# Weight conversion in a fused RWKV-7 and feed-forward kernel: two pieces land in another buffer, six conversion steps stand earlier, nine exponents are made by ScalarE

## The chip, the cores and the metric

The kernel runs on one core of a Trainium2 chip. The metric is the device time of one execution in microseconds (us), the median of the runs shown. The core has five instruction queues that matter here: TensorE (PE, matrix products), VectorE (DVE), ScalarE (ACT), GpSimd (POOL), and SyncE (SP), which issues nearly all DMAs. Each queue works through its instructions in the order written.

## The reference

An RWKV-7 recurrence (4 batches, 8 heads, 768 steps, head size 40) feeds a feed-forward block with a hard-swish (3072 tokens, width 320, hidden 2048):

```
for t in range(S):
    kt, vt, rt = (k[:, :, t], v[:, :, t], r[:, :, t])
    wt, at, bt = (w[:, :, t], a[:, :, t], b[:, :, t])
    y[:, :, t] = np.einsum('bhd,bhde->bhe', rt, state)
    Sa = np.einsum('bhde,bhe->bhd', state, at)
    state_decay = state * wt[:, :, None, :] - np.einsum('bhd,bhe->bhde', Sa, bt)
    state = state_decay + np.einsum('bhd,bhe->bhde', vt, kt)
...
x = np.ascontiguousarray(attn_out.transpose(0, 2, 1, 3)).reshape(B * S, H * D)
h = x @ w_in
relu6 = np.clip(h + 3.0, 0.0, 6.0)
g = h * relu6 / 6.0
return (g @ w_out).astype(np.float32)
```

The six inputs of the recurrence are float32. The two weights `w_in` (320 x 2048) and `w_out` (2048 x 320) arrive as float64, so the kernel has to turn 1.3 million doubles into floats before it can use them.

## The kernel before

**The work.** The sequence is cut into blocks of 64 steps. A *unit* is one block of two batches; there are 24 units (`NK`), handled in groups of four (`NU`). For each unit, preparatory stages (`W`, `gam`, `A`, `B`, `F`, `K`, `factor`, `E`, `EV`) make decay products and score matrices; one inversion per group (`invert`) makes the inverses of many small triangular matrices on VectorE (`prod`, `x`, then the transposes `tb`, `tt`), completed by `third_block` on TensorE (through `zs`) into the tile `tinv`; then the unit's steps (`RT`, `VT`, `C`, `R`, `S`, `U`, `UT`, `rS`, `sn`, `H`, `y`) run the recurrence over the block, and `move`/`move2` carry the result `yg` by DMA into the tile `xt`. The feed-forward reads `xt`: `expand` (L1051, weight `win` and `win2`, products in `h`) and, behind the activation `gt` (ScalarE L1066, VectorE L1067), `contract` (L1092, weight `wout`).

**The conversion.** The weights come in 20 pieces of 128 x 512 doubles, numbered from 0 here; each is 512 KB and is loaded raw as pairs of 32-bit words. `load_weights` is a generator. For piece n it issues, as four steps: (1) the exponent: VectorE keeps the top 12 bits of the high word in the tile `parts` (L349), and two ScalarE instructions make a power of two of them (L350, L352); (2) the product of the piece before, n-1, into its place in `win`, `win2` or `wout` (L360); (3) the mantissa bits of the high word, in place (L369); (4) the low word added (L373). `parts` has two buffers, used in turn. Pieces 0 to 9 are one half of the hidden columns, 10 to 19 the other. The raw words need a home of 1024 words a partition: `raw_homes` lists one for each piece, and for some the number of an earlier piece that must be done before the home is free (`free`). The DMAs of a piece (L327) are issued by SP as soon as its home is free in that sense.

**What sets the order.** The order on every queue is written out by hand. For the first inversion, conversion steps are dealt at fixed steps of the inversion (`STEPS`). The four units of the first group then follow the table `PLAN`: an entry such as `3UT:10` runs stage `UT` of unit 3 and deals ten conversion steps after its matrix products are issued and before its evacuation is; `X` and `Y` are the two halves of the third blocks. What the plan does not deal is dealt in later entries, so the sequence of steps is fixed and the plan only sets what stands between them. The second group's preparation (`by_twos`) begins with the plan's eleventh line.

The lines that matter, as the profile numbers them: L327 raw loads; L349, L350, L352, L360, L369, L373 conversion; L517 masked scores; L541 and L552 scans of the decay; L534 and L538 copies that feed the scans; L954 state update; L980 `ys`; L917 evacuation of `UT`; L880 evacuation of `S`; L995 and L1000 the moves into `xt`; L806 the copies into `tinv`.

Of the kernel before, what the change touches and what calls it, by code (L numbers as in the profile page):

```python
# [7 lines left out]

F32 = mybir.dt.float32
I32 = mybir.dt.int32  # L10
U32 = mybir.dt.uint32
ALU = mybir.AluOpType
AF = mybir.ActivationFunctionType
# [3 lines left out]
P = 128  # L17
BL = 64
# [3 lines left out]
EXP = 916  # L22
# [8 lines left out]
def kernel(  # L31
# [42 lines left out]
    nc = tc.nc  # L74
# [7 lines left out]
    NH = NU * H  # L82
# [4 lines left out]
    const = ctx.enter_context(tc.tile_pool(name="const", bufs=1))  # L87
# [3 lines left out]
    inv = ctx.enter_context(tc.tile_pool(name="inv", bufs=1))  # L91
# [48 lines left out]
    def ps_pair(*dims):  # L140
# [21 lines left out]
        out=ident[:], in_=ones, pattern=[[1, P]],  # L162
# [4 lines left out]
        out=ones[:, 0:BL], in_=ones[:, 0:BL], pattern=[[1, BL]],  # L167
# [3 lines left out]
        out=ones[BL:P, 0:BL], in_=ones[BL:P, BL:P], pattern=[[1, BL]],  # L171
# [6 lines left out]
    nc.vector.memset(three[:], 3.0)  # L178
    warm = const.tile([P, 1], F32, name="warm")
    nc.scalar.activation(out=warm[:], in_=three[:], func=AF.Relu)  # L180
    low = const.tile([P, 2], F32, name="low")
    for i, x in enumerate((EXP - 1792.0, -1792.0 * 2 ** 23)):
        nc.vector.memset(low[:, i:i + 1], x)


# [35 lines left out]
    for i in range(3):  # L221
        t = const.tile([P, H, BL], F32, name=f"score{i}")
# [14 lines left out]
    for p in range(NP):  # L237
        t = const.tile([P, 2, NPR, SLOT], F32, name=f"state{p}")
        nc.vector.memset(t[:], 0.0)
        state.append(t)  # L240
        t = const.tile([P, 2, NPR], F32, name=f"last{p}")
# [16 lines left out]
    for i, (x, y) in enumerate([(0, DFF // 2), (0, NJ // 2)]):  # L258
        for n, z in enumerate((x, y)):
            t = win[:, :, z:z + H * SLOT] if i == 0 else \  # L260
                wout[:, z:z + 4, :].rearrange("p j m -> p (j m)")[:, 0:2 * H * SLOT].rearrange(
                    "p (n x) -> p n x", n=2)
            t = t.rearrange("p n (h e) -> p n h e", e=SLOT)
            name = ("WA", "BK")[i][n]
# [3 lines left out]
    for u in range(2):  # L268
        t = win2[:, u * NPR * P:(u + 1) * NPR * P]
        placed["rgam", 2 + u] = t.rearrange("p (r t) -> p r t", t=P)  # L270
    WC = 256
    PIECES = 20
# [4 lines left out]
    def raw_homes():  # L277


        raws = inv.tile([P, NH, BL], F32, name="raw", tag="F", bufs=2)  # L280
        raws = raws[:].rearrange("p h t -> p (h t)").bitcast(U32)
        places = [raws[:, n * 4 * WC:(n + 1) * 4 * WC] for n in range(2)]
        for j in (NJ // 4, 3 * NJ // 4):
            places.append(wout[:, j:j + NJ // 4, :].rearrange("p j m -> p (j m)")[:, 0:4 * WC].bitcast(U32))
        places = [x.rearrange("p (n c t) -> p n c t", n=2, t=2) for x in places]
        for c in (DFF // 4, 3 * DFF // 4):
            x = win[:, :, c:c + 2 * WC].bitcast(U32)
            places.append(x.rearrange("p n (c t) -> p n c t", t=2))
        x = tinv[:].rearrange("p h t -> p (h t)").bitcast(U32)
        for n in range(2):  # L290
            y = x[:, n * 4 * WC:(n + 1) * 4 * WC]
            places.append(y.rearrange("p (n c t) -> p n c t", n=2, t=2))
        a, b, c, d, e, f, g, h = places
        order = [g, h, a, b, c, d, e, f, a, b, c, d, "x", "fb", "tt", a, b, "fb", "tt", a]
        free = [None] * 8 + [2, 3, 4, 5, None, None, None, 8, 9, 13, 14, 15]
        left = {}
        for n, (x, before) in enumerate(zip(order, free)):
            if isinstance(x, str):
                if x not in left:
                    left[x] = inv.tile([P, L, L], F32, name=f"raw_{x}", tag=x)  # L300
                x = left[x][:].rearrange("p t s -> p (t s)").bitcast(U32)
                x = x.rearrange("p (n c t) -> p n c t", n=2, t=2)
            yield x, before

    def load_weights():

        todo, homes = weight_pieces(), raw_homes()
        loaded, done, issued = deque(), [], [0]
        upcoming = []

        def load():
            if issued[0] == min(PIECES, limit[0]):
                return False
            if not upcoming:
                upcoming.append(next(homes))
            raw, before = upcoming[0]  # L320
            if before is not None and before not in done:
                return False
            upcoming.clear()
            issued[0] += 1
            out, loads = next(todo)
            for to, src in loads(raw):
                nc.sync.dma_start(out=to, in_=src)  # L327
            loaded.append((out, raw))
            return True

        while load():
            pass
        refill.append(load)
        phase[0] = 0
        yield
        before = None
        parts = [grp.tile([P, HD + WPAD], F32, name=f"parts{n}", tag="KBt", bufs=NU + 2)
                 for n in range(2)]
        parts = [t[:, 0:2 * WC].bitcast(U32).rearrange("p (n c) -> p n c", n=2) for t in parts]
        for n in range(PIECES + 1):  # L340
            now = None
            if n < PIECES:
                while load():
                    pass
                out, raw = loaded.popleft()
                hi = raw[:, :, :, 1]
                x = parts[n % 2]
                now = out, raw, x
                nc.vector.tensor_scalar(x, hi, 0xFFF00000, None, ALU.bitwise_and)  # L349
                nc.scalar.activation(out=x.bitcast(F32), in_=x.bitcast(I32), func=AF.Prelu, bias=low[:, 0:1],  # L350
                                     scale=-2.0 ** -20, alpha=2.0 ** -40)
                nc.scalar.activation(out=x.bitcast(I32), in_=x.bitcast(F32), func=AF.Prelu, bias=low[:, 1:2],  # L352
                                     scale=-2.0 ** 63, alpha=2.0 ** -40)
                phase[0] = 1
                yield
            if before:
                to, m, yf = before
                if len(to.shape) == 4:
                    m, yf = (z.rearrange("p n (j c) -> p n j c", c=to.shape[3]) for z in (m, yf))
                nc.vector.tensor_tensor(out=to, in0=m, in1=yf, op=ALU.mult)  # L360
                converted[0] += 1
                done.append(n - 1)
                while load():
                    pass
                phase[0] = 2
                yield
            before = None
            if now:
                nc.vector.tensor_scalar(hi, hi, 0xFFFFF, 0x100000, ALU.bitwise_and, ALU.bitwise_or)  # L369
                phase[0] = 3  # L370
                yield
                m = hi.bitcast(F32)
                nc.vector.scalar_tensor_tensor(m, raw[:, :, :, 0], 2.0 ** -32, hi, ALU.mult, ALU.add)  # L373
                before = out, m, x.bitcast(F32)
                phase[0] = 4
                yield
# [780 lines left out]
    third, F, group_F = [], None, []  # L1157
# [65 lines left out]
    n, cleared = 0, []  # L1223
# [19 lines left out]
    def block(i, j):  # L1243

        if i % NU < 2:
            if j == 0:
# [5 lines left out]

    PLAN = """X X:2 0U:4 0UT:2 1R
              0sn:2 0H:1 Y:2
              1U 1UT:2 0y
              2RT:1 Y:1
              1sn:1 1H:1 2VT:2 0move 0move2
              1y:2 2R
              2S:3 3RT:2
              1move 1move2 2U:3 2UT:1 2C:5  # L1260
# [193 lines left out]
```

## Time and profile before

| | us |
|---|---|
| median of 3 runs | 799.37 (797.80 to 799.43) |
| profiled execution | 800.17 |
| its span, first to last instruction | 798.4 |
| TensorE busy | 734.0 (92%) |
| VectorE busy | 500.5 (63%) |
| ScalarE busy | 307.1 (38%) |
| GpSimd busy | 177.1 (22%) |

The profiled execution is 0.80 us above the median, and 1.8 us of it lie outside its span. TensorE is busy nearly all the time from 140 us on; before that the shares change from stage to stage, so the stages have to be read one by one. A piece of conversion shows in the profile as one line of each of L349, L350, L352, L360, L369 and L373.

### The profile page before, as it was taken

What the parts mean: (1) busy time and instruction counts of PE and PEld (TensorE: products, weight loads), DVE (VectorE), ACT (ScalarE), POOL (GpSimd) and SP (SyncE); (2) the same over time, 40 slices, a digit from 0 to 9 for tenths busy, and PEclk for the clock granted to TensorE, in tenths of its full rate; (3) what the DMA queues carried; (4) which work ended last, traced back from release to release, by engine and by line L of the source; (5) the groups of instructions that cost most, each with busy time, mean ns of one, the idle gap of its engine ahead of it and who ended that gap; (6) DMA issues with size and microseconds to landing.
All of it is one profiled execution on the core that took longest, in us unless ns stands there. A gap on an engine that the chain in (4) does not pass through costs nothing.

```text
span 798.4 us, 35296 instructions
## 1 busy us (share of the span) xinstructions
PE 734.0 (92%) x15832; PEld 624.0 (78%) x15832; DVE 500.5 (63%) x986; ACT 307.1 (38%) x648; POOL 177.1 (22%) x318
## 2 busy tenths in 40 slices
PE   5726778999999989999999999999999999999998
PEld 4625667878778878788888888888888888888886
DVE  7898877689546699445798355888444983323210
ACT  2337653222553424452334454334444324412111
POOL 6403012421223313123214123304222202000000
PEclk9855798999999999999999999999999999999999
DMA  9693653420324322233212223213222101110000
GB/s 122 113 202 87 155 140 55 78 46 9 57 51 72 62 44 39 44 62 59 45 40 42 49 54 63 50 30 62 40 51 45 24 16 29 30 25 13 14 19 17
DMA packets 174214, 45.02 MB, mean 56 GB/s; under 512 B 157424, under 2 KB 172784, under 8 KB 174064
## 3 DMA queue, kind: packets, MB, share of 16 engines
q1 hardware_dynamic: 169760, 42.03, 27.8%
q8 instruction: 125, 2.05, 1.1%
q10 hardware_dynamic: 4304, 0.74, 0.7%
q14 instruction: 25, 0.20, 0.1%
HBM read 34.08 MB, written 3.93 MB: 48 GB/s over the span
## 4 chain that ended last, share of the span: by engine, by line
PE 77%; DVE 8%; issue 5%; SPq 5%; DMA 3%; ACT 1%; POOL 1%; POOLq 0%; DVEq 0%; ACTq 0%
PE h L1051 27%; PE o L1092 23%; PE pair L509 4%; PE pair L969 3%; SPq L455 3%; PE one L471 2%; PE pair L946 2%; PE pair L481 2%; PE pair L853 2%; PE pair L891 2%; PE pair L687 1%; PE pair L911 1%; PE pair L927 1%; PE one L875 1%; SPq L452 1%
## 5 line engine op out<-in xcount | busy, mean ns | idle before, releaser
L1051 PE MATMUL h<-xt,win 128*128 128x128 f32 (+1 forms) x2304 | 252.6, 284 | 3.2 <-DVE gt L1067 2.7
L1051 PEld LDWEIGHTS h<-xt,win 128*128 128x128 f32 (+1 forms) x2304 | 232.9, 193 | 20.6 <-issue 5.4
L1092 PE MATMUL o<-wout,gt 128*128 128x320 f32 x768 | 230.2, 443 | 0.0
L1092 PEld LDWEIGHTS o<-wout,gt 128*128 128x128 f32 x768 | 138.3, 190 | 50.2
L1067 DVE SCALAR_TENSOR_TENSOR gt<-gt,h 128x512 f32<-128x512 f32 x96 | 62.0, 682 | 71.2 <-ACT gt L1066 71.0
L1066 ACT ACTIVATE gt<-h,three 128x512 f32<-128x512 f32 x96 | 62.2, 686 | 101.6 <-PE h L1051 101.2
L981 POOL TENSOR_TENSOR yg<-ys,gam 128x512 f32<-128x512 f32 x22 | 39.7, 1803 | 162.6 <-DVE ys L980 71.8
L738 DVE TENSOR_TENSOR prod<-x 128x30 f32<-128x30 f32 (+9 forms) x180 | 67.2, 373 | 8.8 <-POOL x L723 3.3
L660 POOL TENSOR_TENSOR KBt<-K,rgt 128x320 f32<-128x320 f32 x22 | 19.1, 866 | 212.3 <-ACT rgt L649 207.4
L744 DVE TENSOR_TENSOR x<-x,prod 128x30 f32<-128x30 f32 (+9 forms) x180 | 62.3, 346 | 5.4
L954 DVE TENSOR_TENSOR state<-pair,state 40x320 f32<-40x320 f32 (+1 forms) x44 | 21.4, 487 | 65.5 <-PE pair L946 39.2
L517 DVE COPY_PREDICATED score<-mask,pair 128x512 f32<-128x512 int32 x71 | 50.0, 723 | 1.7 <-PE pair L509 1.2
L980 DVE TENSOR_TENSOR ys<-pair,ys 128x512 f32<-128x512 f32 x22 | 15.2, 690 | 40.9 <-PE pair L687 21.7
L552 DVE TENSOR_TENSOR_SCAN wm<-wm,start 128x528 f32<-128x528 f32 x24 | 37.6, 1566 | 0.8
L541 DVE TENSOR_TENSOR_SCAN prods<-wm,start 128x528 f32<-128x528 f32 x24 | 30.1, 1260 | 10.2 <-ACT wm L538 10.1
L831 ACT ACTIVATE RT<-pair 128x512 f32<-128x512 f32 x21 | 12.5, 597 | 52.8 <-PE pair L481 52.7
L692 ACT ACTIVATE EV<-pair 64x320 f32<-64x320 f32 x44 | 19.0, 432 | 33.7 <-PE pair L687 23.1
L806 ACT ACTIVATE tinv<-pair 32x256 f32<-32x256 f32 x48 | 18.0, 375 | 30.1 <-PE pair L796 29.4
L569 POOL COPY gam<-prods 128x256 f32<-128x256 f32 x24 | 22.5, 938 | 30.6 <-DVE prods L541 26.7
L1110 ACT ACTIVATE ob<-o 128x320 f32<-128x320 f32 x22 | 9.6, 435 | 49.4 <-PE o L1092 29.6
L969 PE MATMUL pair<-score,KBt 64*64 64x64 f32 x1472 | 27.4, 221 | 1.1 <-DVE state L954 0.9
L969 PEld LDWEIGHTS pair<-score,KBt 64*64 64x64 f32 x1472 | 24.0, 134 | 3.7 <-DVE state L954 1.4
(262 smaller groups left out, 1061.6 us busy)
## 6 DMA issues: line engine op xcount, KB each, us to landing
V<-in_v_dram SPq DMA_DIRECT2D x96, 40.0 KB
out_dram<-ob SPq DMA_DIRECT2D x47, 80.0 KB
R<-in_r_dram SPq DMA_DIRECT2D x92, 40.0 KB
B<-in_b_dram SPq DMA_DIRECT2D x42, 80.0 KB
K<-in_k_dram SPq DMA_DIRECT2D x42, 80.0 KB
W<-in_w_dram SPq DMA_DIRECT2D x37, 80.0 KB
A<-in_a_dram SPq DMA_DIRECT2D x37, 80.0 KB
xt<-yg SPq DMA_DIRECT2D x72, 40.0 KB
```

Source lines behind the costliest of these rows:

```text
L509: nc.tensor.matmul(out=o[i][half(q), n, :], lhsT=lhs[half(i, D), n ^ (2 * q * swap), half(q)], rhs=rhs[half(i, D), n, half(q)], start=True ...
L517: nc.vector.copy_predicated(out=x[:].rearrange("p (i h) t -> p i h t", i=2), mask=mask8, data=o[2])
L541: nc.vector.tensor_tensor_scan(out=prods[:].rearrange("p r m i -> p (r m i)"), data0=wm[:, 0:SCAN], data1=start[:], initial=0.0, op0=ALU.m ...
L552: nc.vector.tensor_tensor_scan(out=back, data0=back, data1=start[:], initial=0.0, op0=ALU.mult, op1=ALU.add)
L738: nc.vector.tensor_tensor(out=pv, in0=_ap(x[:], (i + 1) * L + i, [[L, n], [0, i]]), in1=_ap(x[:], i * L, [[0, n], [1, i]]), op=ALU.mult,)
L744: nc.vector.tensor_tensor(out=rest, in0=rest, in1=pv, op=ALU.add)
L969: nc.tensor.matmul(out=y[q][half(s), pr, :], lhsT=o[name][half(q), h * D:h * D + SLOT], rhs=m[name][half(q), 4 * rs + 2 * s + j, :], start ...
L981: nc.gpsimd.tensor_tensor(out=yg[:], in0=m["ys"][:].rearrange("p r q t -> p r (q t)"), in1=o["G"][:], op=ALU.mult)
L1051: nc.tensor.matmul(out=hp[c][:, i, :], lhsT=lhsT, rhs=rhs, start=(begun[c] == 0), stop=(begun[c] == 3 * NQ - 1))
L1066: nc.scalar.activation(out=gt[:], in_=hp[c][:], func=AF.Relu, bias=three[:], scale=1.0)
L1067: nc.vector.scalar_tensor_tensor(out=gt[:], in0=gt[:], scalar=6.0, in1=hp[c][:], op0=ALU.min, op1=ALU.mult)
L1092: nc.tensor.matmul(out=op[:], lhsT=gts[c][:, n, :], rhs=wout[:, c * HJ + r * NQ + n, :], start=((split or r == 0) and c == 0 and n == 0), ...
```

## The change

Three edits, all in the conversion.

1. Pieces 15 and 16 get homes in a new tile `more` that takes the place of the first group's `F`. Pieces 17 and 18 take the two homes in `raw` (free once pieces 8 and 9 are done), piece 19 the home in `fb` (free once piece 13 is done). Before, pieces 15, 16 and 19 were in `raw` (behind 8, 9 and 15), 17 in `fb` (behind 13) and 18 in `tt` (behind 14).
2. In the plan, three conversion steps are dealt behind the products of `y` of unit 0 (before: none), and four behind those of `sn` of unit 1 (before: one).
3. For pieces 0 to 3 and 15 to 19, ScalarE makes the exponent field itself: it reads the top 16 bits of each double as an integer, multiplies by 1/16 and subtracts 15/32, and writes the result as an integer into `parts`. The VectorE instruction L349 of these pieces goes.

```
-    low = const.tile([P, 2], F32, name="low")
-    for i, x in enumerate((EXP - 1792.0, -1792.0 * 2 ** 23)):
+    low = const.tile([P, 3], F32, name="low")
+    for i, x in enumerate((EXP - 1792.0, -1792.0 * 2 ** 23, -15.0 / 32.0)):
...
-        order = [g, h, a, b, c, d, e, f, a, b, c, d, "x", "fb", "tt", a, b, "fb", "tt", a]
-        free = [None] * 8 + [2, 3, 4, 5, None, None, None, 8, 9, 13, 14, 15]
+        order = [g, h, a, b, c, d, e, f, a, b, c, d, "x", "fb", "tt", 0, 1, a, b, "fb"]
+        free = [None] * 8 + [2, 3, 4, 5, None, None, None, None, None, 8, 9, 13]
...
+            if isinstance(x, int):
+                if x == 0:
+                    more = inv.tile([P, NH, BL], F32, name="more", tag="F", bufs=2)
+                    more = more[:].rearrange("p h t -> p (h t)").bitcast(U32)
+                x = more[:, x * 4 * WC:(x + 1) * 4 * WC].rearrange("p (n c t) -> p n c t", n=2, t=2)
...
-                nc.vector.tensor_scalar(x, hi, 0xFFF00000, None, ALU.bitwise_and)
+                fine = 2.0 ** -20
+                if n < 4 or n >= PIECES - 5:
+                    fine = 1.0
+                    top = raw.rearrange("p n c t -> p n (c t)").bitcast(I16)[:, :, 3::4]
+                    nc.scalar.activation(out=x.bitcast(I32), in_=top, func=AF.Identity, bias=low[:, 2:3],
+                                         scale=1.0 / 16.0)
+                else:
+                    nc.vector.tensor_scalar(x, hi, 0xFFF00000, None, ALU.bitwise_and)
                 nc.scalar.activation(out=x.bitcast(F32), in_=x.bitcast(I32), func=AF.Prelu, bias=low[:, 0:1],
-                                     scale=-2.0 ** -20, alpha=2.0 ** -40)
+                                     scale=-fine, alpha=2.0 ** -40)
...
-              1U 1UT:2 0y
+              1U 1UT:2 0y:3
...
-              1sn:1 1H:1 2VT:2 0move 0move2
+              1sn:4 1H:1 2VT:2 0move 0move2
```

The order of TensorE's and GpSimd's instructions is the same in both kernels. VectorE has nine conversion instructions fewer and one constant more, ScalarE nine activations more. SP issues the loads of pieces 15 to 17 ahead of unit 0's move, piece 18 behind it and piece 19 behind unit 1's, where before piece 15 followed unit 0's move, piece 16 unit 1's, and 17 to 19 came behind the first loads for the second group.

More of the change, by code (lines that the diff above doesn't have):

```diff
@@ L9 @@
 F32 = mybir.dt.float32
+I16 = mybir.dt.int16
 I32 = mybir.dt.int32
```

## The prediction

> **What bounds the kernel now.** I read the page's slices first, then TensorE's timeline from 60 to 135 us, then VectorE's and ScalarE's for what ends each gap, then the stretches of 1 us for the granted clock.
>
> ```profile
> PE   5726778999999989999999999999999999999998
> DVE  7898877689546699445798355888444983323210
> ACT  2337653222553424452334454334444324412111
> PEclk9855798999999999999999999999999999999999
> ```
>
> Each digit is 20 us. From the eighth slice on TensorE is full at full clock; nothing in the change touches that part, so time can only be won or lost before about 135 us and is then carried to the end. In slices three to seven VectorE is nearly full and TensorE's clock is low. TensorE's last waits in this stage (start, duration, then the wait and its releaser):
>
> ```profile
> 108.39 1.16 PE L1051 MATMUL h<-xt,win 128*128 128x128 f32 x8 [2.06 <-DVE gt L1067]
> 113.16 0.69 PE L911 MATMUL pair<-tinv,RR 64*64 64x64 f32 x32 [2.07 <-DVE ys L980]
> 121.93 1.08 PE L471 MATMUL pair<-ident,WA 128*128 128x128 f32 x4 [3.60 <-issue]
> 131.41 1.34 PE L969 MATMUL pair<-score,KBt 64*64 64x64 f32 x64 [0.87 <-DVE state L954]
> ```
>
> Three of the four are the conversion's doing. VectorE waits for a raw piece with `ys` behind it, and again for the next:
>
> ```profile
> 111.14 0.43 DVE L349 TENSOR_SCALAR parts<-raw 128x512 uint32<-128x512 uint32 x1 [2.21 <-DMA raw<-in_moe_w_out_dram]
> 112.41 0.69 DVE L980 TENSOR_TENSOR ys<-pair,ys 128x512 f32<-128x512 f32 x1
> 115.24 0.43 DVE L349 TENSOR_SCALAR parts<-raw_fb 128x512 uint32<-128x512 uint32 x1 [1.54 <-DMA raw_fb<-in_moe_w_out_dram]
> 122.83 2.39 DVE L541 TENSOR_TENSOR_SCAN prods<-wm,start 128x528 f32<-128x528 f32 x2
> ```
>
> And ScalarE reaches `UT` of unit 3, whose bank the product at 121.93 needs (that is the "issue" wait), only behind the last piece:
>
> ```profile
> 120.62 0.72 ACT L352 ACTIVATE parts<-parts,low 128x512 int32<-128x512 f32 x1
> 121.25 0.58 ACT L917 ACTIVATE UT<-pair 128x512 f32<-128x512 f32 x1
> ```
>
> From 122.83 VectorE then runs without a break to the score at 131.26: two scans, two more (L552), `gt`, `state`. It sets the product at 131.41. So the figure to forecast is when that scan chain starts.
>
> **Part by part.**
>
> *Pieces 0 to 3.* Each loses a L349 worth 0.33 us of VectorE's pitch (39.22 to 39.56) and adds 0.74 us on ScalarE (pitch of L350 to L352, 50.68 to 51.42). The new read is of 16-bit integers with a stride; no row has that. Bounds: the contiguous 32-bit row of the same 512 elements, 0.72 us, and twice that, 1.44 us, if the stride cost a second pass. I take 0.72, the nearest row. Two savings vanish: L369 of piece 1 now has to wait until ScalarE has read the high words (50.68 + 0.72 = 51.40, against L369 at 51.43 before), and the score at 52.13 already waited 0.28 us for products that hang on the load of `R`. So only piece 2's 0.33 us reaches the transposes at 62.18. Piece 3's new activation then stands on ScalarE ahead of the copies into `tinv` (L806, 69.13), which release the next products: 69.13 - 0.33 + 0.74 = 69.54. This edit makes TensorE 0.41 us later from 70.4 on.
>
> *The plan's six steps.* They fill VectorE's waits of 1.97 us (before 79.92) and 2.62 us (before 84.91). Ahead of the first come L369, L373 and L349, 1.3 us; ahead of the second, with what stood there, work that ends at 84.3 against products ready at 85.3. Both fit. On ScalarE piece 7's two activations pass ahead of `RT` of unit 2 and the second L806 (+1.2 us, not needed until 89.8). The rest of the conversion is 4.6 us of VectorE's idle time nearer its end. In my walk through the queues, ScalarE's `RT` of unit 2 (behind piece 11) makes the products at 93.55 start at 94.45, but `U` no longer waits, so the feed-forward starts at 97.5 for 97.17: +0.33.
>
> *The loads.* Pieces 15 to 17 (512 KB each) go ahead of unit 0's move on SP: three issues of some 0.5 us each, and SP starts 0.4 later, so the move ends its first four issues at 94.1 for 92.2. The transfers ahead hold 1.5 MB; at the 300 to 380 GB/s of the busiest stretches that is 4 to 5 us from 90, so `xt` lands near 96.5, 1 us before it is read. The waits of 2.21 and 1.54 us for raw pieces go. SP is later by 2 us for piece 19 (107.3); with the 5 us that raw pieces took (105.6 to 111.1) it lands at 113, needed at 113.9. The loads for unit 5 follow by 112.3, in place of 110.2, needed at 118.6.
>
> *Pieces 15 to 19 on ScalarE.* A piece is now 0.75 + 0.75 + 0.65 = 2.15 us there. Piece 15 starts at 101.6 (behind `VT`), then `ys` at 103.75, piece 16 to 106.4, piece 17 to 108.6, `S`, and only then `gt` at 109.1, which started at 106.93 before. Queued behind the pieces: `gt` on VectorE and the products at 108.39, now 110.35. This is the price, 2.0 us, and TensorE is idle from 106.7: 3.7 us.
>
> Then it pays. VectorE is through piece 16 by 107.3 and stands free: `ys` follows its products at once. TensorE at half clock from 110.4: 4.0 us for `h` and `score`, `ys` done at 114.95, `UT`'s products at 115.0 (113.16 before, all still late by 1.85). But ScalarE does piece 18 from 110.3, `U`, piece 19 from 113.9, and `UT` at 116.1 in place of 121.25. TensorE goes through to 118.65 without a gap and takes the product of 121.93 there, at full clock: done at 119.25. The copy for the second scan (L538) follows at 119.95, the second scan starts at 120.0 for 124.03 and the chain behind it is 4.05 us earlier: `state` at 126.8, the product of 131.41 at 127.35.
>
> *The clock.* The rows that decide it:
>
> ```profile
> 111.00:112.00 1.00, 0.08 (x8) 0.00 (x0) 0.86 (x2) 0.40 (x1) 0.00 (x0) 1.00 0.94 124
> 112.00:113.00 1.00, 0.00 (x0) 0.00 (x0) 1.00 (x3) 0.97 (x3) 0.00 (x0) 1.00 0.66 163
> 114.00:115.00 1.00, 1.00 (x26) 0.88 (x17) 0.00 (x0) 0.00 (x0) 0.83 (x1) 0.50 1.08 383
> 121.00:122.00 1.00, 0.07 (x1) 0.10 (x2) 0.90 (x2) 1.00 (x4) 0.00 (x0) 0.50 0.00 0
> ```
>
> The second and third numbers are TensorE's busy time and its weight loads'; the last three are granted clock, DMA share, GB/s. The clock changes at 93.4, 100.2, 113.9, 117.2, 120.8 and 127.4, all near multiples of 3.4 us apart, and falls after a stretch of that length with 1.0 to 1.4 us of work; with 2.0 us it held once (107 to 110.4) and fell once (at 172). After the change TensorE, fast, has done its work by 124.5 and waits 2.85 us for `state`; the stretch 124.1 to 127.5 holds 0.5 us of work, so I expect half clock to 130.9: 1.7 us lost.
>
> Sum: -4.05 + 1.7 = -2.35 us. The profiled execution would be 797.8; taken from the median, 799.37 - 2.35 = 797.0.
>
> The Trainium skill (TensorE: Matmul & The Clock Gate, section "HAM oscillation") gives the rule that no idle gap should exceed about 3.4 us. By it the 2.85 us gap would cost nothing and the time would be 795.3; but the trace lost the clock at 113.9 after gaps no longer than 2.07 us, and the row decides.
>
> **The rivals.**
>
> *The clock holds* at 127.5: -4.05, 795.3. For it: 1.5 us more of work in that stretch may be enough (2.0 us held it once). Against: the gap is long.
>
> *The clock eats it*: a stretch with 2.3 us of work (93.4 to 96.8) did not bring the clock back, so half clock may last two stretches, 3.4 us: -0.65, 798.7. The change also would come to this if `more` held up `xt`.
>
> *Slower: ScalarE's queue.* If the strided 16-bit activation takes 1.44 us, piece 3 delays `tinv` by another 0.72, and pieces 15 to 17 delay `gt` by 2.2 more; the products of 108.39 start at 113.2 or later, at half clock to 117.2, and the product of 121.93 is taken at 122.0 to 122.7. The scans gain 0.7 us or nothing, and the half clock behind them still costs 1.7 to 3.4: +1.0 to +2.7, middle +1.9, 801.3. It decides from about double the price of the 32-bit row. For it: `gt` has no slack against pieces 16 and 17. Against: nothing in L350 to L352 hints at a price by type (0.72 for integers in and for integers out).
>
> That the change does not act is excluded by the order of instructions: VectorE's nine L349 are gone, and the loads stand earlier.
>
> **Numbers.** Forecast 0.45, the clock holding 0.16, eating 0.17, ScalarE's queue 0.22. About 0.2% (1.6 us) is what a measurement of this kernel can tell from no change. Faster by more than that: the first two, less a little of the forecast's lower edge, 0.58; within: 0.20; slower: 0.22. The range runs from 794.4, a little beyond the clock holding, to 801.3, the middle of the slower case.
>
> **What would show it.** Right: no L349 wait for DMA behind 105 us; new activations of 0.72 us; `gt` on ScalarE near 109; `UT` of unit 3 near 116; the second scan near 120; half clock behind 127.5. Wrong: new activations well over 0.75 us; waits of `h` for `xt` at 97.5; `UT` later than 119; a product of 131.41 that does not come before 130.

## The result, and the profile after

| | before | after |
|---|---|---|
| median, us (22 runs each) | 799.21 | 801.67 |
| lowest and highest | 796.76, 801.13 | 797.83, 806.24 |
| profiled execution | 800.17 | 801.73 |
| its span | 798.4 | 799.9 |

The ratio is 1.0028, with a 95% interval of 1.0017 to 1.0038: 2.2 us slower (the two medians lie 2.5 us apart), where I had forecast 2.4 us faster and gave "slower" 0.22. The changed kernel also scatters more (8.4 us from lowest to highest, against 4.4).

The changed kernel's lines are numbered some 13 higher (L1051 is now L1064, L541 is L554, L954 is L967, L980 is L993, L969 is L982); L359 is the new activation, L382 and L386 the mantissa steps, L373 the product. The slices of the page, 20 us each:

```profile
PE   5725787999999989999999999999999999999998
DVE  7897876689445699445798355888444973322210
ACT  2347771322553424452334454234444324412111
PEclk9855689999999999999999999999999999999999
```

The clock is lower than before in the fifth and sixth slice (6 for 7, 8 for 9) and higher in the seventh (9 for 8). The timeline of TensorE (start, duration, line, tiles; in brackets the idle time ahead and what ended it):

```profile
100.97 4.32 PE L1064 MATMUL h<-xt,win 128*128 128x128 f32 x24 [2.92 <-DMA xt<-yg]
...
112.75 1.16 PE L1064 MATMUL h<-xt,win 128*128 128x128 f32 x8 [2.67 <-DVE gt L1080]
...
120.32 0.60 PE L484 MATMUL pair<-ident,WA 128*128 128x128 f32 x4
...
130.88 1.77 PE L982 MATMUL pair<-score,KBt 64*64 64x64 f32 x64 [4.16 <-DVE state L967]
```

The wait of 3.60 us for `UT` is gone: the product with `WA` starts at 120.32 in place of 121.93. But there is a new wait of 2.92 us for `xt`, the one for `gt` is 2.67 us in place of 2.06, and the 1.6 us won at 120.32 are spent waiting for `state`, 4.16 us for 0.87. VectorE's timeline has the reason:

```profile
112.01 1.28 DVE L1080 SCALAR_TENSOR_TENSOR gt<-gt,h 128x512 f32<-128x512 f32 x2 [1.74 <-ACT gt L1079]
...
115.65 0.69 DVE L993 TENSOR_TENSOR ys<-pair,ys 128x512 f32<-128x512 f32 x1 [1.29 <-DMA raw_fb<-in_moe_w_out_dram]
...
116.86 1.52 DVE L382 TENSOR_SCALAR raw<-raw 128x512 uint32<-128x512 uint32 x1
...
122.30 2.39 DVE L554 TENSOR_TENSOR_SCAN prods<-wm,start 128x528 f32<-128x528 f32 x2
```

No wait for a raw piece is left, as forecast, though the name of one stands at 115.65: there `ys` waited for the `score` products, which ran at half clock from 113.84 to 115.60. The scans start at 122.30, 0.53 us earlier than before and not 4.05. ScalarE:

```profile
108.66 0.75 ACT L359 ACTIVATE parts<-raw,low 128x512 int32<-128x512 int16 x1
...
111.30 1.26 ACT L1079 ACTIVATE gt<-h,three 128x512 f32<-128x512 f32 x2
...
119.16 0.58 ACT L930 ACTIVATE UT<-pair 128x512 f32<-128x512 f32 x1
```

The new activation takes 0.75 us; `gt` starts behind it and its two followers at 111.30 (forecast 109.1), `UT` at 119.16 (116.1). The stretches of 1 us behind the new gap (TensorE's busy time is the second number, the granted clock the third from the end):

```profile
127.00:128.00 1.00, 0.00 (x0) 0.00 (x0) 0.97 (x3) 0.00 (x0) 0.69 (x4) 1.00 0.34 59
131.00:132.00 1.00, 1.00 (x48) 1.00 (x52) 0.46 (x1) 0.00 (x0) 0.00 (x0) 0.61 0.22 74
```

Behind the gap the clock is half from 131.2 to 134.6, a stretch of the length forecast.

### The profile page after: what moved, and what is told of

Same layout as the page of the kernel before. It is cut to its first block, busy times and chain, and to the rows that moved or that the text cites. A ratio compares the mean times of both kernels' runs of the same rounds, so it can differ in the third digit from the quotient of the medians.

```text
span 799.9 us, 35306 instructions
## 1 busy us (share of the span) xinstructions
PE 732.5 (92%) x15832; PEld 622.1 (78%) x15832; DVE 498.8 (62%) x978; ACT 313.4 (39%) x657; POOL 175.6 (22%) x318
## 4 chain that ended last, share of the span: by engine, by line
PE 72%; DVE 11%; SPq 6%; issue 5%; DMA 3%; ACT 1%; POOL 1%; POOLq 0%; DVEq 0%; ACTq 0%
PE h L1064 24%; PE o L1105 22%; PE pair L522 4%; PE pair L982 3%; PE pair L494 2%; PE one L484 2%; PE pair L959 2%; DVE prod L751 2%; DVE x L757 2%; SPq L468 2%; SPq L465 2%; PE pair L904 2%; PE pair L866 1%; DVE prods L554 1%; PE pair L924 1%
## 5 line engine op out<-in xcount | busy, mean ns | idle before, releaser
L1064 PE MATMUL h<-xt,win 128*128 128x128 f32 (+1 forms) x2304 | 249.2, 282 | 6.2 <-DVE gt L1080 3.3
L1064 PEld LDWEIGHTS h<-xt,win 128*128 128x128 f32 (+1 forms) x2304 | 229.6, 191 | 23.5 <-issue 7.5
L967 DVE TENSOR_TENSOR state<-pair,state 40x320 f32<-40x320 f32 (+1 forms) x44 | 21.4, 487 | 65.0 <-PE pair L959 38.4
L993 DVE TENSOR_TENSOR ys<-pair,ys 128x512 f32<-128x512 f32 x22 | 15.2, 690 | 43.6 <-PE pair L700 22.1
L565 DVE TENSOR_TENSOR_SCAN wm<-wm,start 128x528 f32<-128x528 f32 x24 | 37.5, 1564 | 0.8
L554 DVE TENSOR_TENSOR_SCAN prods<-wm,start 128x528 f32<-128x528 f32 x24 | 30.7, 1286 | 10.5 <-ACT wm L551 10.5
L982 PE MATMUL pair<-score,KBt 64*64 64x64 f32 x1472 | 29.1, 231 | 4.9 <-DVE state L967 4.2
L982 PEld LDWEIGHTS pair<-score,KBt 64*64 64x64 f32 x1472 | 25.6, 143 | 7.4 <-DVE state L967 4.7
```

The costliest lines, as they stand in the source:

```text
L554: nc.vector.tensor_tensor_scan(out=prods[:].rearrange("p r m i -> p (r m i)"), data0=wm[:, 0:SCAN], data1=start[:], initial=0.0, op0=ALU.m ...
L565: nc.vector.tensor_tensor_scan(out=back, data0=back, data1=start[:], initial=0.0, op0=ALU.mult, op1=ALU.add)
L982: nc.tensor.matmul(out=y[q][half(s), pr, :], lhsT=o[name][half(q), h * D:h * D + SLOT], rhs=m[name][half(q), 4 * rs + 2 * s + j, :], start ...
L1064: nc.tensor.matmul(out=hp[c][:, i, :], lhsT=lhsT, rhs=rhs, start=(begun[c] == 0), stop=(begun[c] == 3 * NQ - 1))
```

## The experiments

Every ratio is to the kernel before, run beside it on the same chip; it is not exactly the ratio of two medians. "Marker" is the first transpose of `A` on TensorE (`one<-ident,A`), behind which TensorE is full: 134.93 before, 135.84 after.

| run | what it is | median, us | ratio, 95% interval |
|---|---|---|---|
| e1 | edit 1 alone (homes) | 799.02 | 1.0007 [0.9995, 1.0020] |
| e2 | edit 2 alone (early steps) | 803.40 | 1.0059 [1.0043, 1.0075] |
| e3 | edit 3 alone (exponents) | 800.08 | 1.0024 [1.0010, 1.0037] |
| e7 | edits 1 and 3 | 801.01 | 1.0008 [0.9989, 1.0027] |
| e8 | edits 1 and 2 | 800.91 | 1.0022 [1.0007, 1.0037] |
| e4 | after, unit 0's move ahead of raw loads | 803.35 | 1.0058 [1.0039, 1.0078] |
| e9 | after, shorter queue behind `ys` | 798.94 | 0.9989 [0.9970, 1.0008] |
| e11 | after, again | 801.81 | 1.0031 [1.0014, 1.0048] |
| e6 | after + L | 799.51 | 1.0004 [0.9990, 1.0018] |
| e10 | after + G | 800.99 | 1.0027 [1.0011, 1.0042] |
| e5 | after + S | 800.23 | 1.0013 [0.9994, 1.0032] |
| e16 | after + L + G | 797.56 | 0.9983 [0.9969, 0.9997] |
| e14 | after + L + S | 795.57 | 0.9956 [0.9936, 0.9976] |
| e15 | after + G + S | 796.44 | 0.9972 [0.9958, 0.9986] |
| e12 | after + L + G + S | 792.53 | 0.9922 [0.9902, 0.9943] |
| e13 | before + S | 799.65 | 1.0005 [0.9989, 1.0021] |
| e17 | e12 without edit 3 | 794.55 | 0.9948 [0.9933, 0.9964] |
| e18 | e12 without edit 2 | 798.42 | 0.9997 [0.9985, 1.0009] |

L: the first four exponents go back to VectorE. G: `gt` ahead of piece 17 on ScalarE. S: unit 3's `state` between the two pairs of scans. The theories in the expectations have letters of their own, which are not these.

**The edits one at a time (e1, e2, e3).** Each is its part of the diff above. Three theories: X, the raw loads ahead of the move hold up `xt`; Y, the new exponents stand on ScalarE ahead of `gt`; Z, the six early steps delay TensorE through ScalarE.

> Edit 1 alone (the new homes of pieces 15 to 19; plan and exponents as before). The changed kernel took 801.67 us against 799.21 before, and in its trace TensorE waited 2.92 us at 100.97 us for xt of unit 0, whose moves were issued behind the raw loads of pieces 15 to 17. Theory X (the moves are late behind raw loads): two loads of 512 KB now stand ahead of the move, so a wait of h for xt of 1 to 2 us at about 98 us, the raw-piece waits of VectorE (2.21 and 1.54 us) gone, time 799.5 to 801.5. Theory Y (ScalarE's exponents ahead of gt are the loss): without them the new homes only take VectorE's waits away, time 796.5 to 798.5, no wait for xt. Theory Z (the six steps dealt earlier delay TensorE through ScalarE): as Y for this kernel.

> Edit 2 alone (the six conversion steps behind y of unit 0 and sn of unit 1; homes and exponents as before). Theory X: no loads are moved much, so 798 to 799.5, with RT of unit 2 and the second copies into tinv later on ScalarE by about 1.2 us and nothing waiting for them. Theory Y: the same, 798 to 799.5. Theory Z: piece 7's two activations ahead of RT and of the copies into tinv make SP and TensorE late by 1 us or more at 90 us, time 800.5 to 802.

> Edit 3 alone (nine exponents by ScalarE; homes and plan as before). Theory X: no wait for xt is added; piece 3's activation costs 0.4 us at the first copies into tinv, the tail changes little because VectorE still waits for raw pieces: 799 to 800. Theory Y: the exponents of the last pieces stand ahead of gt and of UT on ScalarE and cost 2 us or more: 801 to 803. Theory Z: 799 to 800.

Edit 1 alone is no different from before. Edit 2 alone is the worst, and for a reason that none of the three names. VectorE's timeline of e2:

```profile
111.65 0.43 DVE L349 TENSOR_SCALAR parts<-raw_fb 128x512 uint32<-128x512 uint32 x1 [4.84 <-DMA raw_fb<-in_moe_w_out_dram]
```

With the old homes, the early steps bring the exponent of piece 17 in front of `gt` while its load has not come. That is a cost of edit 2 without edit 1, not of the change. In e3 the last five exponents wait on ScalarE for the late loads, and their three activations a piece (2.15 us) set the pace of the conversion:

```profile
112.80 0.75 ACT L354 ACTIVATE parts<-raw,low 128x512 int32<-128x512 int16 x1 [2.79 <-DMA raw<-in_moe_w_out_dram]
...
117.45 0.76 ACT L354 ACTIVATE parts<-raw_fb,low 128x512 int32<-128x512 int16 x1 [2.07 <-DMA raw_fb<-in_moe_w_out_dram]
```

**The move ahead of the raw loads (e4).**

```
         if t == 3:
-            limit[0] = PIECES
+            limit[0] = 15
+        if t == 4:
+            limit[0] = PIECES
```

> The changed kernel with one thing taken back: the limit on loads is 15 until unit 0's move is issued, so pieces 15 to 18 are loaded behind that move and no longer ahead of it (homes, plan and exponents stay). Theory X: unit 0's move ends about 2 us earlier on SP and its data no longer lie behind 1.5 MB, so the wait of h for xt (2.92 us) falls below 0.5 us, and the time falls by 2 to 3 us against the changed kernel, to 798.5 to 799.7. Theory Y: gt stays behind pieces 16 and 17 on ScalarE, or later because the loads are later: 801 to 802.5. Theory Z: unchanged, 801 to 802.

TensorE's timeline:

```profile
98.52 5.49 PE L1064 MATMUL h<-xt,win 128*128 128x128 f32 x24 [0.68 <-ACT UT L930]
...
130.81 1.99 PE L982 MATMUL pair<-score,KBt 64*64 64x64 f32 x64 [4.62 <-DVE state L967]
```

The wait for `xt` is gone (0.68 us, for `UT`), and the scans still start at 122.24 and the wait for `state` is still there. So X falls as the cause: `xt` was late, but its cure is worth nothing here. Why this kernel is 0.3% slower than the changed one is open. Its trace has half clock from 111.5 to 114.9, 128.5 to 135.4 and 173.0 to 176.4, 6.8 us of full clock lost in all, against 3.4 us behind 110 us in the changed kernel's; that is one trace of each.

**The edits in pairs (e7, e8).** Theory V is that the gain is eaten behind 100 us, on VectorE's queue.

> Edits 1 and 3 without edit 2 (the plan as it was). Edit 3 alone was 1.9 us slower than before, and its trace has waits of 2.79 and 2.07 us of ScalarE for raw pieces, which the new homes would take away. Theory V: without those waits the conversion is bound by ScalarE's 2.15 us a piece at its end, the scans start near 122.5, and the time is 798.5 to 800. Rival (the exponents cost by their place ahead of S and gt, whatever the loads do): as slow as edit 3 alone, 800 to 801.5.

> Edits 1 and 2 without edit 3 (all exponents on VectorE). Edit 2 alone was 4.6 us slower: its earlier steps put the exponent of piece 17 on VectorE in a wait of 4.84 us for a raw load with gt behind it. If the new homes cure just that, the time is 797.5 to 799.5, and edit 3 is what costs in the changed kernel (about 2 to 3 us); if the early steps cost by themselves (gt behind pieces 16 and 17 on ScalarE, xt behind the raw loads), it is 800 to 803 and edit 3 is neutral or a gain beside it.

The new homes take 0.37% off edit 2 (1.0059 to 1.0022): they cure the wait for piece 17. But homes and early steps together still cost 0.2%, without edit 3. e7 is inconclusive, its runs lie between 797.0 and 803.7.

**State between the scans (e5, S).** The second group's first step issues only the first scans (L554); the second scans (L565) follow an entry of the plan later, behind unit 3's `state` and masked score. On TensorE 24 products of `h` move behind unit 3's.

```
-                order = [0, 1, 0, 1][4 * t:]
+                order = [0, 1]
```

> The changed kernel with one change in the order: the second group's first step issues only the decay scans (L554), and the second scans (L565) with the gam products follow one entry of the plan later, so that unit 3's state and masked score stand between the two pairs of scans. Theory V (the gain was eaten on VectorE's queue: unit 3's state stands behind both pairs of scans, and these behind the conversion): state moves from 130.34 to about 125, the product that waited 4.16 us for it starts near 125.5 in place of 130.88, and the half clock behind that gap goes too; TensorE's marker (the first transpose of A, 135.84) comes at 130.5 to 133, and the time falls by 3 to 5 us against the changed kernel, to 797 to 799 and below the kernel before. Theory G (TensorE's second-group work needs the second scans, so the wait only moves): the marker stays within 1 us of 135.84, a new wait for gam or the products behind it of 2 to 4 us appears, and the time is within 1.5 us of the changed kernel's.

The wait for `state` went from 4.16 us to none and the marker came at 131.92, as V expects (130.5 to 133); the time fell by 0.15% only, and its interval takes in both theories. Neither was settled by this run alone.

**The first four exponents (e6, L).**

```
-                if n < 4 or n >= PIECES - 5:
+                if n >= PIECES - 5:
```

> The changed kernel, but pieces 0 to 3 keep their exponents on VectorE (only the last five are ScalarE's). My prediction had the first four cost 0.41 us of TensorE's time from 70 us on. Theory V (all the loss is behind 100 us): within 0.8 us of the changed kernel. Theory E (ScalarE's extra activations ahead of the copies into tinv and of RT set the time at 70 to 100 us, where TensorE was already 2 us late at 90 us): TensorE is 1 to 2.5 us earlier at 97 us and the time falls by as much.

It takes off 0.24%, 1.9 us: the time is as theory E has it, and V, as an account of the whole loss, falls. E's other sign did not come: the transposes of `V` start at 96.30 in place of 96.99, 0.7 us earlier and not 1 to 2.5.

**A shorter queue behind `ys` (e9).** L382 and L386 of pieces 18 and 19 are left out.

```
-                nc.vector.tensor_scalar(hi, hi, 0xFFFFF, 0x100000, ...)
+                if n < PIECES - 2:
+                    nc.vector.tensor_scalar(hi, hi, 0xFFFFF, 0x100000, ...)
...
-                nc.vector.scalar_tensor_tensor(m, raw[:, :, :, 0], ...)
+                if n < PIECES - 2:
+                    nc.vector.scalar_tensor_tensor(m, raw[:, :, :, 0], ...)
```

> The changed kernel without the mantissa instructions (L382, L386) of pieces 18 and 19; it leaves those two pieces unconverted, and nothing else. Behind ys of unit 2 VectorE then has 3.2 us less to do before the scans (1.52 + 0.80 and 0.42 + 0.79 by the changed kernel's rows, 3.5, less what the slow instruction beside GpSimd passes on to its neighbour). Theory Q (the forecast failed only because the pieces queued behind ys were left out of the walk: the scans start a fixed 6.65 us behind ys): the scans start 3 to 3.6 us earlier against ys, near 119, state near 127, and the time falls as the forecast's sum has it, by 2.4 to 3.6 us against the changed kernel, to 798 to 799. Theory G (what stands behind the scans is limited by something else, half clock or DMA): scans at 119, and the time within 1 us of the changed kernel's.

The median is 2.9 us below that of the changed kernel beside it (e11: 798.94 to 801.81), as theory Q has it. In this trace, though, the queue shrank by less than that. VectorE shows where the rest of the 3.2 us stayed:

```profile
117.68 0.69 DVE L995 TENSOR_TENSOR ys<-pair,ys 128x512 f32<-128x512 f32 x1 [0.71 <-DMA WA<-in_a_dram]
118.29 2.37 DVE L373 TENSOR_TENSOR wout<-raw,parts 128x512 f32<-128x512 f32 x2
121.33 0.69 DVE L373 TENSOR_TENSOR wout<-raw_fb,parts 128x512 f32<-128x512 f32 x1 [0.67 <-ACT parts L365]
...
122.56 2.40 DVE L556 TENSOR_TENSOR_SCAN prods<-wm,start 128x528 f32<-128x528 f32 x2
```

From `ys` to the scans are 4.88 us in place of 6.65, 1.8 less and not 3 to 3.6: the product of piece 19 now waits 0.67 us for ScalarE, and the slow instruction is now L373 (two take 2.37 us, one takes 0.69). That the median fell by more than 1.8 us is not explained. This execution also waited 4.84 us at 102.91, so its absolute times say nothing.

**`gt` ahead of piece 17 (e10, G).**

```
-              2rS:3 2sn:3 2H:4 3S:2
-              2y:3 3U:1 3UT:10 3C:5
+              2rS:3 2sn:3 2H:4 3S
+              2y:5 3U:1 3UT:10 3C:5
```

> The changed kernel with two conversion steps moved from S of unit 3 to y of unit 2, so that ScalarE evacuates S and does gt before the exponent of piece 17, not behind it. Theory Y (piece 17's 2.2 us on ScalarE ahead of gt is what delays the products, ys and so the scans): gt starts 1.2 to 2.2 us earlier than 111.30 (bounded by the expand products, which ended at 110.1), ys and the scans as much earlier, and the time falls by 1 to 2 us. Rival (the pieces need the same ScalarE time either way; UT of unit 3 moves back to where it was, or ys still waits for its products): the scans within 0.6 us of 122.3 and the time unchanged.

The start of `gt` on ScalarE, and of the scans on VectorE:

```profile
109.77 1.27 ACT L1079 ACTIVATE gt<-h,three 128x512 f32<-128x512 f32 x2 [0.68 <-PE h L1064]
```

```profile
120.18 2.39 DVE L554 TENSOR_TENSOR_SCAN prods<-wm,start 128x528 f32<-128x528 f32 x2
```

And TensorE:

```profile
128.76 1.99 PE L982 MATMUL pair<-score,KBt 64*64 64x64 f32 x64 [3.66 <-DVE state L967]
```

`gt` is 1.5 us earlier and the scans 2.1, as Y expects, but the median is that of the changed kernel. `state` still stands behind both pairs of scans, TensorE waits 3.66 us for it, and the clock is half from 127.3 to 134.1. That this gap ate the gain is likely (e15 takes it away, and is 0.55% faster) but not shown by this trace: it is of the fastest of the twelve runs, 797.31, so its instants cannot be set against a median of 800.99.

**The same kernel again (e11).**

> The changed kernel once more, on this call's chip, for a second trace of the same code and twelve more times. If the places of the half-clock windows and the waits for instructions are fixed by the code, TensorE's marker (first transpose of A, 135.84), the scans (122.30) and the wait of 4.16 us return within 0.3 us; if they fall anew in each execution, the marker moves by 1 us or more while the distance from ys to the scans stays 6.65 us. Median 800.5 to 802.5.

```profile
114.02 0.69 DVE L993 TENSOR_TENSOR ys<-pair,ys 128x512 f32<-128x512 f32 x1 [0.70 <-DMA WA<-in_a_dram]
...
120.67 2.39 DVE L554 TENSOR_TENSOR_SCAN prods<-wm,start 128x528 f32<-128x528 f32 x2
```

The same code has `ys` at 114.02 and the scans at 120.67 (115.65 and 122.30 in the first trace), its `xt` wait is 1.42 us for 2.92, and its half clock lies at 127.5 to 134.4 for 131.2 to 134.6. The absolute times scatter by 0.9 us (the marker, at 134.99) to 1.6 (the scans); the distance from `ys` to the scans, 6.65, does not. In every trace with edit 2 it is 6.62 to 6.79 (e9, which leaves work out, aside).

**All three put right (e12), and each left out (e14, e15, e16).**

> The changed kernel with three things put right: exponents of pieces 0 to 3 back on VectorE, gt ahead of piece 17 on ScalarE, and unit 3's state and masked score between the two pairs of decay scans. By the runs so far the first was worth 1.9 us and the third 1.2 us (0.28 to 0.04 and 0.13% above the kernel before), the second 1 to 2 by theory Y. If these add up, 796 to 797.5, about 0.3% below the kernel before; if the first and third were scatter of the clock's windows, 799 to 801.

> The changed kernel with the first four exponents back on VectorE and the scans' order changed, but gt still behind piece 17 on ScalarE. Singly the two were worth 1.9 and 1.3 us. If they add, 798 to 799; if the clock decides (no gap of over 2 us is left behind 101 us, so the half-clock windows of 114 to 117 and 127 to 134 both go), 793 to 796; theory Y (gt ahead of piece 17 is needed, since S waits for the masked score behind the pieces): over 797.5.

> The changed kernel with gt ahead of piece 17 and the scans' order changed; the first four exponents stay on ScalarE. Theory E (the first four exponents are worth 1.9 us or more, by the copies into tinv): 794.5 to 797. Theory N (the first four are neutral, their 1.0 us gain on VectorE and 0.8 us loss ahead of tinv cancel): 791.5 to 794, as the best version.

> The changed kernel with the first four exponents back on VectorE and gt ahead of piece 17, but state behind both pairs of scans. Theory Q (state's wait of 3.7 to 4.6 us, with the half clock behind it, is what takes the gain): the wait stays at 3.5 to 4.6 us, half clock behind 127, 798.5 to 800.5. If the order of the scans adds nothing by itself: 792 to 795.

e12 is 0.78% faster than before and 1.1% faster than the change, below the 796 to 797.5 that adding up single gains had given (six runs, all between 791.2 and 796.0). VectorE and TensorE of e12:

```profile
117.61 2.39 DVE L554 TENSOR_TENSOR_SCAN prods<-wm,start 128x528 f32<-128x528 f32 x2
119.92 0.47 DVE L967 TENSOR_TENSOR state<-pair,state 128x320 f32<-128x320 f32 x1
```

```profile
117.77 0.70 PE L940 MATMUL pair<-RT,S 40*64 40x64 f32 x32 [0.67 <-DVE score L530]
...
123.32 1.16 PE L982 MATMUL pair<-score,KBt 64*64 64x64 f32 x64
...
126.67 0.60 PE L484 MATMUL one<-ident,A 128*128 128x128 f32 x4
```

The scans start at 117.61, `state` follows 2.31 us behind them and not 8.04, and no gap of over 0.8 us is left on TensorE between 110 and 150 us; the clock is full from 101.4 to beyond 200. The marker is 8.3 us ahead of the kernel before.

Each thing was added to four kernels, so its worth can be read four times (differences of ratios). L: 0.24, 0.44, 0.57 and 0.50%, mean 0.44%, 3.5 us. S: 0.15, 0.48, 0.55, 0.61%, mean 0.45%. G: 0.01, 0.21, 0.41, 0.34%, mean 0.24%. One such difference is uncertain by 0.2 to 0.3%. All three are least with the changed kernel as it stands and more beside another, and together they bring 1.06% where their single worths add to 0.40%; that excess, 0.66%, is uncertain by some 0.4%. My reading is that each closes a gap behind which the clock can fall. The traces fit it for S: in all five that have S beside edit 2 (e5, e12, e14, e15, e17) the clock is full from 110 to 150 us, and in the other fifteen 1.7 to 6.8 us of it are lost there. In e14 the expected 793 to 796 of the clock's theory came (795.57), in e15 those of theory E (796.44). In e16 theory Q was right on the wait (3.67 us for `state`) and missed the time by 0.9 us, with one stretch of half clock behind it and not two.

**Are the edits needed (e13, e17, e18)?** e13 is S on the kernel before; e17 is e12 with every exponent on VectorE; e18 is e12 with the old plan, in which `gt` stands ahead of piece 16 already.

> The kernel before with only the decay scans' order changed (state and masked score of unit 3 between the two pairs of scans), none of the three edits. Theory S (the order of state and scans alone is worth the 6.6 us; the three edits add nothing): 791.5 to 794.5. Theory Q (in the kernel before the conversion ends late and the product waits only 0.87 us for state, so there is little to win without the edits): 797.5 to 799.5, at most 1.5 us below the kernel before.

> The best version without edit 3: all exponents on VectorE (new homes, earlier steps, gt ahead of piece 17, state between the scans). If edit 3's last five exponents are needed (they take 5 x 0.33 us from VectorE's queue, of which those of pieces 18 and 19 lie behind ys), it is 0.7 to 2.5 us slower than the best version, 793.5 to 795. If the exponents of the last five are neutral too, 792 to 793.5.

> The best version without edit 2: new homes, the last five exponents on ScalarE, state between the scans, and the plan as it was (gt then stands ahead of piece 16 already). If the six early steps are what shortens the queue behind ys once the rest is right, it is 2 us or more slower than the best version, 795 to 798; if the early steps only move waits, 792 to 794.

S on the kernel before does nothing. Its TensorE shows why, as theory Q has it:

```profile
121.12 1.09 PE L471 MATMUL pair<-ident,WA 128*128 128x128 f32 x4 [4.50 <-issue]
...
131.00 1.16 PE L969 MATMUL pair<-score,KBt 64*64 64x64 f32 x64
```

`state` is ready at 125.5, but TensorE comes to the product only at 131.00, without a wait: it stood 4.50 us at 121.12 (as before, for `UT`, which ScalarE evacuates behind the last piece), and its work was then late by itself. The same wait is back in e18, without the six early steps:

```profile
120.40 1.08 PE L484 MATMUL pair<-ident,WA 128*128 128x128 f32 x4 [3.94 <-issue]
```

So edit 2, the worst alone (+0.59%), is worth 0.75% in the repaired kernel (e18 against e12), and edit 3, without its first four pieces, 0.26% (e17 against e12; I gave 0.7 to 2.5 us, and it is 2.1). The second figure is just as large as its uncertainty. Edit 1 was not left out of the repaired kernel.

## Why the prediction was wrong

**The step that failed: from `ys` to the second scan.** The prediction had `ys` done at 114.95, `UT` at 116.1, its product at 119.25 and "the second scan starts at 120.0". It followed `UT`'s side, ScalarE and TensorE, and left out VectorE's own queue: between `ys` and the scans stand the product of piece 17, three instructions each of pieces 18 and 19, and the masked score, in strict order. In the trace of after:

0.61 (`ys`) + 0.60 + 1.55 + 0.80 + 0.61 + 0.46 + 0.79 + 0.61 + 0.62 = 6.65 us.

From the start of my `ys`, 114.35, that gives the first scan at 121.0 and the second at 122.2, where I wrote 120.0: 2.2 us of the 4.05 were never there. e11 (the same distance in another execution) and e9 (shorten this queue, and the scans come nearer to `ys` and the time falls) show it.

Half of this is in one line. L382 of piece 18 took 1.52 us at 116.86, where others take 0.42. Beside it GpSimd runs:

```profile
116.48 1.61 POOL L994 TENSOR_TENSOR yg<-ys,gam 128x512 f32<-128x512 f32 x1 [9.24 <-DMA WA<-in_w_dram]
```

Before, the same GpSimd instruction ran at 113.23, mostly in VectorE's wait for piece 17. The wait that the change removed had hidden it. In each of the other 19 traces the VectorE instruction that begins while this one runs, whichever stands there, ends 0.28 to 0.55 us after it: L382 of after, the product in e3 (1.58 us for 0.69), the second product in e9. The Trainium skill (SBUF — State Buffer, section "SBUF: two separate sides") says that VectorE and GpSimd take a shared pair of ports as a lock, and that the loser is blocked for the whole instruction; on VectorE's side it names instructions in a two-port mode or with two inputs in SBUF. The traces agree for the products, which have two inputs; that L382, which has one, uses both ports is not shown, and no run took the GpSimd instruction away.

**The price ahead of `ys`, mis-sized.** I had `gt` at 109.1, 2.2 us later than before; it came at 111.30, 4.4 later (110.25 in e11). `xt` was to land 1 us early and came 2.92 us late in this trace, 1.42 in the next. SyncE's issues of unit 0's move, in after and then in e11:

```profile
94.58 3.22 SPq L1008 DMA_DIRECT2D xt<-yg  x4
```

```profile
90.39 3.22 SPq L1008 DMA_DIRECT2D xt<-yg  x4
```

I had the first four issues end at 94.1 and `xt` land 2.4 us behind them. In after they ended at 97.80; in e11 they ended at 93.61, and `h` still waited for them until 99.17, 5.6 us behind. So the landing was priced too low, and in the first trace the queue was late too. In e4, where nothing waited for `xt`, `gt` came at 110.45, so ScalarE's queue, without a break there from 102.50 on, is most of what was late. `ys` was 1.3 us later than my walk. With the 2.2 us above, 4.05 - 2.2 - 1.3 = 0.55 us are left; the trace has 0.53.

**From the scans to `state`: right, and overlooked as a choice.** I had this chain 4.05 us earlier as a whole. It did stay as long as before (8.04 us, 8.03 before). But that `state` is queued behind scans that it does not need was in the lines I read, and the gap in front of it was the price of winning at `UT`. e12 against e16 shows that taking `state` out is worth 0.6%.

**The clock.** The forecast term (1.7 us) came in the first trace, the rival's (two stretches) in the second; that the first one matched was luck.

**The slower rival's sum.** Its upper end leaves out a case that its own terms allow: no gain at the scans and 3.4 us of half clock make +3.4, not +2.7, so the middle would have been +2.2 and 801.6, not 801.3. The time came near it, but by VectorE's queue and not by the rival's condition: the new activation took 0.75 us.

**Pieces 0 to 3, mis-sized.** I had TensorE 0.41 us later from 70.4. In the four pairs with and without L (after and e11 averaged), the products with `tinv` start 0.6 us later with the exponents on ScalarE (0 to 1.5), which is about my term. But by the transposes of `V` near 97 us the pairs are 2.2 us apart (0.5 to 3.9), and the times 3.5 us. Part of what lies between may be the clock: summing 1 minus the granted clock from 74 to 94 us, in these pairs the kernels with the four exponents lose 4.5 to 8.1 us and those without 1.7 to 6.2. Over all 20 traces the two groups overlap more, 3.2 to 8.1 (mean 6.4) against 1.7 to 7.4 (mean 4.5), so that the clock carries the loss is likely and not shown. The stretches from 80 to 82 us of after, and then of e12:

```profile
80.00:82.00 2.00, 1.49 (x50) 1.46 (x49) 0.00 (x0) 1.65 (x3) 0.00 (x0) 0.50 0.50 131
```

```profile
80.00:82.00 2.00, 0.34 (x14) 0.28 (x10) 1.97 (x6) 1.98 (x5) 0.00 (x0) 1.00 0.88 223
```

I priced a delay of 0.41 us as 0.41 us in a stage where the clock stood at half and had yet to rise. Why a shift of half a microsecond holds it down so long is not shown by these runs.

**What stays open.** With the start of the scans as it came, my sum would have been -0.55 + 1.7 = +1.2 us; the runs have 2.2 to 2.5. The marker came 0.9 us later than before in the first trace and 0.1 us in the second. From the marker to the end the 20 traces take 660.6 to 665.2 us, so with a trace or two of each kernel the rest cannot be placed.

**What was right.** The price of the new activation (0.72 forecast, 0.75 to 0.77 measured), so the rival of a second pass falls; the end of VectorE's waits for raw pieces; `gt` late through ScalarE's queue; the earlier `UT`; the half clock behind a gap at `state`. "A product of 131.41 that does not come before 130" stood as the sign of a wrong forecast, and it came at 130.88. That the edits can give the time is shown too, but only with L, G and S: 0.78% below before.

## What to carry to other kernels

Walk every engine's queue in order to the instruction you are pricing, and end the sum only where the last of them arrives; a wait that falls on one engine is worth no more than the queue that stands behind the next instruction on the other. Before crediting a removed wait, list what ran on other engines inside it, and what the waiting engine's next consumer is queued behind without need. And judge an edit within the set it belongs to: the one that cost most alone was, of the two that were left out in turn, the one that gained most once what stood behind it was moved.

## What the runs showed of the hardware that I had not expected

**The clock's windows lie elsewhere in each execution.** Half clock comes in stretches of 3.4 us or multiples, but where the stretches begin is not fixed by the code (e11). So a gap may or may not cost it. Near 170 us all kernels have a wait for the same `score`, 1.45 to 1.61 us in 18 of the 20 traces (2.46 in e4, 0.81 in e18). Before:

```profile
170.72 0.68 PE L687 MATMUL pair<-V,score 64*64 64x40 f32 x32 [1.46 <-DVE score L517]
```

```profile
172.00:173.00 1.00, 1.00 (x3) 0.28 (x1) 0.97 (x4) 0.33 (x1) 0.00 (x0) 0.50 0.61 102
```

and e12:

```profile
163.88 0.67 PE L700 MATMUL pair<-V,score 64*64 64x40 f32 x32 [1.49 <-DVE score L530]
```

```profile
166.00:167.00 1.00, 1.00 (x36) 0.95 (x37) 0.93 (x4) 0.31 (x1) 0.00 (x0) 1.00 0.75 119
```

Behind it the first had half clock for 3.4 us, the second full clock; so it went in ten traces and in ten. The rule of the Trainium skill that I weighed in the prediction (TensorE: Matmul & The Clock Gate, section "HAM oscillation": no idle gap over about 3.4 us) is too mild: half clock followed 1.46 us of waiting here. And the same wait of 2.67 us ahead of `h` was followed by half clock in after, at 114.1, and by full clock in e11. The clock goes with the scatter of one code (standard deviation 2.1 us over the 22 runs of after): the three fastest runs were granted 0.961 of it in the mean, five of the six slowest 0.944 to 0.949. That it makes all of the scatter is not shown. A single trace is one draw.

**Waits of TensorE that no engine releases.** Between 74 and 96 us every trace has 1.6 to 5.6 us of waits put down to "issue", mostly in the middle of a group of equal products. The longest is not the same in each execution of one code, as after and then e11 show:

```profile
80.51 1.65 PE L982 MATMUL lent<-score,KBt 64*64 64x64 f32 x50 [1.75 <-issue]
```

```profile
83.43 0.77 PE L959 MATMUL pair<-V,KBt 64*64 64x40 f32 x20 [1.83 <-issue]
```

But the places are fixed. Between 70 and 100 us, in all 20 traces, these waits stand ahead of the same five products only, 126 to 128 products apart: the 976th in the trace, the 1103rd, the 1230th, the 1358th and the 1484th. What changes is which of them wait, and how long. I left these out of the walk. That the instructions themselves come late there is my reading of "issue"; the even spacing fits it, and no run tested it.
